# Squared-ReLU MLP on one core: a new start (x in partition halves, first matmuls on half the columns) and blocks in the order A0 A1 B0 A2 B1 A3 B2 B3

## The chip, the core and the metric

The kernel runs on one core of a Trainium2 chip. TensorE (PE in the profile, with PEld for its weight loads) does all matrix products, ScalarE (ACT) and VectorE (DVE) move results out of PSUM, GpSimd (POOL) prepares constants, and SyncE (SP) issues most transfers. The metric is the device time of one execution, in microseconds (us). Lower is better. The kernel before has a median of 292.39 us over three runs (292.11 to 292.75).

## The reference

```python
# B, S, D, F = 1, 2048, 576, 4608; all bf16
h = jnp.einsum("bsd,df->bsf", x, w1) + b1
r = jnp.where(h > 0, h, 0)
out = jnp.einsum("bsf,fd->bsd", r * r, w2) + b2
```

Two matrix products with a squared ReLU between them. Each has 2048 x 576 x 4608 multiply-adds.

## The kernel before, in words

**Blocks and phases.** The 2048 rows of x are cut into four blocks (0 to 3) of 512 rows. For each block, phase A computes the hidden layer transposed: `hT` has 128 partitions, 36 column tiles of F (the loop variable `ft`) and 512 rows of x. Phase B multiplies it with w2 into four row tiles of 128 rows by 576 columns, as two halves of 288 columns, adds b2 and writes them out. Two `hT` buffers exist (`hpool`, L51). The order of the phases is written out by hand at the end of the function (L275 to L291): A0 A1 B0 B1 A2 A3 B2 B3.

**Phase A has two kinds of matmul.** D = 576 is four and a half times 128. For the first four column tiles of F (`a_full`, L180), four matmuls use the whole array with a contraction of 128 (`full`, L194), and the last 64 rows of D are done by two matmuls that run side by side on the lower and upper 64 rows of the array (`pair`, L188 and L190). For the other 32 column tiles (`a_rows`, L164) everything is done by such pairs, with nine contractions of 64 each: L173 on the lower half, L175 on the upper half. Call the first kind full-array and the second kind half-array matmuls. Phase B (L233) is full-array, with 288 columns. In A0 the full-array part comes first and goes contraction by contraction over four PSUM banks (`"k_outer"`, L205); in A1 and A3 the half-array part comes first and `a_full` follows (`"rows_first"`, L197); in A2 `a_full` comes first, bank by bank (`"g_outer"`, L211).

**Transposed x.** Phase A needs x transposed (`xT`, nine windows of 64 or 128 partitions). Blocks 1 to 3 get it by transposing transfers (L120, L121). Block 0 gets it on TensorE: four row tiles `x_sb` are loaded, each is transposed in five 128 x 128 pieces (three into `ta`, L138, two into `tb`, L141 and L142); DVE copies `ta` (L139) and ACT copies `tb` (L143, L144) into `xT`. The first window used, O, is written by DVE's copy; `dup_windows` (L113, L114) then copies windows to the other half of the partitions.

**The start.** TensorE first runs warm-up matmuls on a constant (L61): six of 512 columns and one of 256. SP issues x row tile 0 and x row tile 2, ACT issues row tiles 1 and 3 (L83 to L86, by `load_x`, L70). SP then issues the four parts of `w1n` (L73, the weights of the full-array part of A, one for each contraction `k`), and after them the stream of `w1_h` (L80, w_h in the profile: the weights of the half-array part, first one column tile for each half, then two at a time), the transposing loads of block 1, more of `w1_h`, b2 and w2. POOL makes the identity for the transposes, loads b1 (L94) and then the two halves of `w1n8` (L77, w1n_89 in the profile: the 64 last rows of D for the first four column tiles). All instructions are kept in program order on each engine (`keep`), so TensorE does the 20 transposes of the four row tiles before the first matmul of A0. The transpose of b1 (L151) stands after contraction k = 1 of A0.

**PSUM.** Eight banks: four in `ps_h` (the transposes `ta`, the half-array results, two of the four `a_full` banks) and four in `ps_o` (`tb`, the other two `a_full` banks, phase B). ACT takes an A result out with the ReLU and b1 (L161), DVE squares it into `hT` (L162). DVE adds b2 to a B result (L242), and SP writes it out (L261, the last two halves by L254).

Of the kernel before, what the change touches and what calls it, by code (L numbers as in the profile page):

```python
# [17 lines left out]
def kernel(  # L18
# [9 lines left out]
    nc = tc.nc  # L28
    keep = tc.keep_in_program_order
    P = 128  # L30
    H = 64
    x2 = x.flatten_outer_dims()
# [5 lines left out]
    NK = NC // 2  # L38
    G = 4
# [4 lines left out]
    SB = 512  # L44
# [11 lines left out]

    wps = ps_o.tile([P, 512], FP32, name="wps", tag="po")
    ones = nc.const_aps.tensor(1.0, [P, 512], BF16)
    WARM = [512] * 6 + [256]
    for i, n in enumerate(WARM):  # L60
        keep(nc.tensor.matmul(wps[:, 0:n], lhsT=ones[:, 0:P], rhs=ones[:, 0:n], start=True, stop=True))  # L61

    xs = const.tile([P, RT, D], BF16, name="x_sb")
    w1n = wpool.tile([P, NK, GW], BF16, name="w1n")
    w1n8 = wpool.tile([P, G // 2, P], BF16, name="w1n8")
    w1_h = wpool.tile([P, NC, FH], BF16, name="w1_h")
    w1_v = w1.rearrange("(c p) f -> p c f", p=H)

    def load_x(eng, rt):
        keep(eng.dma_start(out=xs[:, rt, :], in_=x2[rt * P:(rt + 1) * P, :]))  # L70

    def load_w1n(eng, k):
        keep(eng.dma_start(out=w1n[:, k, :], in_=w1[k * P:(k + 1) * P, 0:GW]))  # L73

    def load_w1n8(eng, h):
        src = w1[NK * P:D, 0:GW].rearrange("p (i h f) -> p i h f", h=2, f=P)
        keep(eng.dma_start(out=w1n8[h * H:(h + 1) * H, :, :], in_=src[:, :, h, :]))  # L77
# [2 lines left out]
        keep(eng.dma_start(out=w1_h[h * H:(h + 1) * H, :, j0 * P:j1 * P],  # L80
                      in_=w1_v[:, :, GW + h * FH + j0 * P:GW + h * FH + j1 * P]))

    load_x(nc.sync, 0)  # L83
    load_x(nc.scalar, 1)
    load_x(nc.sync, 2)
    load_x(nc.scalar, 3)  # L86
    for k in range(NK):
        load_w1n(nc.sync, k)

    ident = const.tile([P, P], BF16, name="ident")  # L90
    make_identity(nc, ident[:])
    b1_rows = const.tile([P, P], BF16, name="b1_rows")
    nc.gpsimd.memset(b1_rows[:], 0.0)
    nc.gpsimd.dma_start(out=b1_rows[0:NFT, :], in_=b1.rearrange("(ft p) -> ft p", p=P))  # L94
    load_w1n8(nc.gpsimd, 0)
    load_w1n8(nc.gpsimd, 1)
    warm = const.tile([P, 1], FP32, name="warm")
    keep(nc.scalar.activation(out=warm[:], in_=nc.const_aps.tensor(0.0, [P, 1], FP32), func=ACT.Relu))  # L98

    E3, O, SPC, E = 0, 1, 5, 6  # L100
# [53 lines left out]
    hTs = {}  # L154

    def alloc_hT(sb):
        hTs[sb] = hpool.tile([P, NFT, SB], BF16, name="hT", tag="hT")
# [6 lines left out]
    def a_rows(sb, dup_at=None, dup_sb=None):  # L164
        xT = xT_blk[sb]
        for j in range(NJ):
            if j == dup_at:
                dup_windows(dup_sb)
            bx = ps_h.tile([P, SB], FP32, name="ph", tag="ph")
            by = ps_h.tile([P, SB], FP32, name="ph", tag="ph")  # L170
            jc = slice(j * P, (j + 1) * P)
            for i in range(NC):
                keep(nc.tensor.matmul(bx[:], lhsT=w1_h[0:H, LO_C[i], jc], rhs=xT[0:H, LO_W[i], :],  # L173
                                 start=(i == 0), stop=(i == NC - 1)))
                keep(nc.tensor.matmul(by[:], lhsT=w1_h[H:P, UP_C[i], jc], rhs=xT[H:P, UP_W[i], :],  # L175
                                 start=(i == 0), stop=(i == NC - 1)))
            evac_h(sb, bx, G + j)
            evac_h(sb, by, G + NJ + j)

    def a_full(sb, order):  # L180
        xT = xT_blk[sb]
        banks = []
        for g in range(G):
            pool, tag = (ps_o, "po") if g < 2 else (ps_h, "ph")
            banks.append(pool.tile([P, SB], FP32, name="pn", tag=tag))

        def pair(i, start, stop):
            keep(nc.tensor.matmul(banks[2 * i][:], lhsT=w1n8[0:H, i, :], rhs=xT[0:H, SPC, :],  # L188
                             start=start, stop=stop))
            keep(nc.tensor.matmul(banks[2 * i + 1][:], lhsT=w1n8[H:P, i, :], rhs=xT[H:P, E3, :],  # L190
                             start=start, stop=stop))

        def full(g, k, start, stop):
            keep(nc.tensor.matmul(banks[g][:], lhsT=w1n[:, k, g * P:(g + 1) * P], rhs=xT[:, O + k, :],  # L194
                             start=start, stop=stop))

        if order == "rows_first":  # L197
            for i in (1, 0):
                pair(i, True, False)
            for g in (2, 3, 0, 1):  # L200
                for k in range(NK):
                    full(g, k, False, k == NK - 1)
                evac_h(sb, banks[g], g)
        else:
            if order == "k_outer":  # L205
                for k in range(NK):
                    for g in range(G):
                        full(g, k, k == 0, False)
                    if k == 1:
                        make_b1T()  # L210
            else:  # L211
                for g in (2, 3, 0, 1):
                    for k in range(NK):
                        full(g, k, k == 0, False)
            for i in (1, 0):
                pair(i, False, True)
                evac_h(sb, banks[2 * i], 2 * i)
                evac_h(sb, banks[2 * i + 1], 2 * i + 1)
# [5 lines left out]
    def phase_b(sb, hT, last=False, dups=()):  # L224
        for jj in range(RT):
            if jj < len(dups):
                dup_windows(dups[jj])
            rt = sb * RT + jj
            po = [ps_o.tile([P, 512], FP32, name="po", tag="po") for _ in range(2)]
            o_sb = opool.tile([P, D], BF16, name="o_sb", tag="o_sb")  # L230

            def mmb(i, ft, h):
                keep(nc.tensor.matmul(  # L233
                    po[h][:, 0:DH],
                    lhsT=hT[:, ft, jj * P:(jj + 1) * P],
                    rhs=w2_sb[:, ft, h * DH:(h + 1) * DH],
                    start=(i == 0),
                    stop=(i == NFT - 1),
                ))

            def evac(h):
                keep(nc.vector.tensor_tensor(  # L242
                    out=o_sb[:, h * DH:(h + 1) * DH],
                    in0=po[h][:, 0:DH],
                    in1=b2_bc[:, h * DH:(h + 1) * DH],
                    op=ALU.add,
                ))

            if last and jj == RT - 1:
                for h in range(2):  # L250
                    for i, ft in enumerate(ft_order):
                        mmb(i, ft, h)
                    evac(h)
                    keep(nc.sync.dma_start(out=out2[rt * P:(rt + 1) * P, h * DH:(h + 1) * DH], in_=o_sb[:, h * DH:(h + 1) * DH]))  # L254
                continue
            for i, ft in enumerate(ft_order):
                for h in range(2):
                    mmb(i, ft, h)
            for h in range(2):
                evac(h)  # L260
            keep(nc.sync.dma_start(out=out2[rt * P:(rt + 1) * P, :], in_=o_sb[:]))  # L261
# [18 lines left out]
    a_rows(1)  # L280
    a_full(1, "rows_first")
    phase_b(0, hTs[0], dups=(2, 3))
    phase_b(1, hTs[1])
    alloc_hT(2)
    a_full(2, "g_outer")
    a_rows(2)
    alloc_hT(3)
    a_rows(3)
    a_full(3, "rows_first")
    phase_b(2, hTs[2])  # L290
    phase_b(3, hTs[3], last=True)  # L291

# [29 lines left out]
```

## Time and profile before

| what | value |
| --- | --- |
| median of three runs | 292.39 us (292.11 to 292.75) |
| the profiled execution, own time | 292.11 us |
| its span | 290.3 us, so 1.8 us lie outside the span |
| PE busy | 285.7 us, 2409 recorded matmuls |
| ACT busy, DVE busy | 94.2 us, 81.5 us |
| first matmul of the program (warm-up) | 0.78 us |
| first transpose of x | 3.51 us |
| first full-array matmul of A0 (L194) | 5.71 us |
| first half-array matmul of A0 (L173) | 9.75 us |
| last matmul ends | 287.3 us |

The profile's page has the busy time of each engine, the span in 40 slices, the chain of work that ended last, the costliest groups of instructions by line, and the transfers. Besides the page, the timeline (instructions in order of time; neighbours of one line are merged, "x3" means three), a table of busy time and transferred bytes by stretch of time, and the list of transfers with their time from issue to landing are used below. In the timeline a line holds start, duration, engine, source line, operation, tiles and the number of merged instructions; in brackets the idle time of that engine before it and what ended it. Matmuls overlap in the pipeline: the distance from one start to the next is the pace, the duration of one is longer. A few matmul records are missing in a trace: 61 of the 64 of L194 are there.

### The profile page before, as it was taken

To read this page: it belongs to the slowest core of one execution; us is meant where nothing else is said; L and a number is where in the kernel's file an instruction comes from. 1 tells how busy PE (TensorE), PEld (TensorE's weight loads), DVE (VectorE), ACT (ScalarE), POOL (GpSimd) and SP (SyncE) were. 2 spreads that over 40 slices of the span, in tenths; PEclk is the share of its full clock that TensorE was granted. 3 is DMA by queue.
4 is the path that set the end of the run, shared out by engine and by line. 5 is a ranking of instruction groups with operands and counts; after the bars stand their busy time and mean duration, and the time that the engine had idled before them with its cause. 6 is when DMAs were issued, how large, how long until landed. Compare 5 with 4: busy or idle time off the path is not lost.

```text
span 290.3 us, 5455 instructions
## 1 busy us (share of the span) xinstructions
PE 285.7 (98%) x2409; PEld 178.0 (61%) x2412; DVE 81.5 (28%) x189; ACT 94.2 (32%) x154; POOL 2.7 (1%) x10
## 2 busy tenths in 40 slices
PE   8999999999999999999999999999999999999995
PEld 4444444444677777777744444444447777777774
DVE  3344544444531011110025444444440111100111
ACT  4566666666400000000027666666670000000000
POOL 3000000000000000000000000000000000000000
PEclk9999999999999999999999999999999999999999
DMA  7999999900000000000000000000000000000000
GB/s 203 214 212 177 255 357 265 164 1 2 0 23 0 23 20 20 23 3 20 20 23 0 3 0 2 0 2 0 2 0 2 20 24 20 21 2 23 20 20 24
DMA packets 27096, 16.05 MB, mean 55 GB/s; under 512 B 11028, under 2 KB 27040, under 8 KB 27072
## 3 DMA queue, kind: packets, MB, share of 16 engines
q1 hardware_dynamic: 26688, 15.32, 23.9%
q8 instruction: 19, 0.31, 0.4%
q10 hardware_dynamic: 288, 0.30, 0.3%
q0 software_dynamic: 96, 0.07, 0.1%
q14 instruction: 5, 0.04, 0.0%
HBM read 11.36 MB, written 2.36 MB: 47 GB/s over the span
## 4 chain that ended last, share of the span: by engine, by line
PE 98%; ACT 0%; issue 0%; DVE 0%
PE po L233 49%; PE ph L173 42%; PE pn L194 5%; PE wps L61 1%; PE ph L175 1%; PE pn L188 1%; PE ta L138 0%; ACT xTw L143 0%; DVE o_sb L242 0%; ACT xTw L144 0%; PE tb L141 0%; PE tb L142 0%; PE b1T_ps L151 0%; PE pn L190 0%
## 5 line engine op out<-in xcount | busy, mean ns | idle before, releaser
L233 PE MATMUL po<-w_sb,hT 128*128 128x288 bf16 x1152 | 141.4, 286 | 0.0
L233 PEld LDWEIGHTS <-hT 128*128 128x128 bf16 x1152 | 112.7, 98 | 28.8
L173 PE MATMUL ph<-xTw,w_h 64*128 64x512 bf16 x576 | 124.6, 376 | 0.0
L175 PE MATMUL ph<-xTw,w_h 64*128 64x512 bf16 x576 | 124.6, 376 | 0.0
L173 PEld LDWEIGHTS <-w_h 64*128 64x128 bf16 x576 | 54.1, 94 | 68.3
L161 ACT ACTIVATE r<-ph,b1T 128x512 bf16<-128x512 f32 x128 | 81.1, 685 | 41.6 <-PE ph L175 41.6
L162 DVE TENSOR_TENSOR hT<-r 128x512 bf16<-128x512 bf16 x144 | 61.2, 426 | 77.3 <-ACT r L161 76.7
L175 PEld LDWEIGHTS <-w_h 64*128 64x128 bf16 x576 | 54.1, 94 | 0.0
L242 DVE TENSOR_TENSOR o_sb<-po,b_bc 128x288 bf16<-128x288 f32 x32 | 13.3, 453 | 123.9 <-PE po L233 123.9
L161 ACT ACTIVATE r<-pn,b1T 128x512 bf16<-128x512 f32 x16 | 10.3, 688 | 78.8 <-PE pn L190 77.5
L194 PE MATMUL pn<-xTw,w1n 128*128 128x512 bf16 x61 | 14.0, 379 | 0.8 <-ACT xTw L143 0.4
L194 PEld LDWEIGHTS <-w1n 128*128 128x128 bf16 x64 | 6.0, 98 | 8.0 <-issue 1.4
L61 PE MATMUL wps<-const-bfloat16-1.0 128*128 128x512 bf16 (+1 forms) x7 | 2.9, 594 | 0.8 <-PEq L306 0.8
L113 DVE COPY xTw<-xTw 64x2048 bf16<-64x2048 bf16 x4 | 2.8, 690 | 0.4 <-ACT xTw L144 0.3
L114 DVE COPY xTw<-xTw 64x2048 bf16<-64x2048 bf16 x4 | 2.7, 687 | 0.1
L139 DVE COPY xTw<-ta 128x384 bf16<-128x384 bf16 x4 | 1.3, 358 | 4.2 <-PE ta L138 4.2
L188 PE MATMUL pn<-xTw,w1n_89 64*128 64x512 bf16 x8 | 2.4, 379 | 0.0
L190 PE MATMUL pn<-xTw,w1n_89 64*128 64x512 bf16 x8 | 2.4, 379 | 0.0
L61 PEld LDWEIGHTS <-const-bfloat16-1.0 128*128 128x128 bf16 x7 | 0.9, 135 | 2.1 <-issue 2.1
L98 ACT ACT_TABLE_LOAD x1 | 1.3, 1283 | 1.7 <-PEq L306 1.7
L138 PE MATMUL ta<-ident,x_sb 128*128 128x128 bf16 x12 | 1.6, 265 | 0.0
L143 ACT COPY xTw<-tb 128x128 bf16<-128x128 bf16 x4 | 1.1, 282 | 1.2 <-PE tb L142 1.1
(21 smaller groups left out, 10.2 us busy)
## 6 DMA issues: line engine op xcount, KB each, us to landing
w_sb<-in_w_dram SPq DMA_DIRECT2D x6, 864.0 KB, 11.4
w_h<-in_w_dram SPq DMA_DIRECT2D x14, 288.0 KB, 7.4
out_dram<-o_sb SPq DMA_DIRECT2D x15, 144.0 KB, 1.8
w_h<-in_w_dram SPq DMA_DIRECT2D x4, 144.0 KB, 4.1
w1n<-in_w_dram SPq DMA_DIRECT2D x4, 128.0 KB, 4.0
x_sb<-in_x_dram ACTq DMA_DIRECT2D x2, 144.0 KB, 3.0
x_sb<-in_x_dram SPq DMA_DIRECT2D x2, 144.0 KB, 2.8
b_bc<-in_b_dram SPq DMA_DIRECT2D x1, 144.0 KB, 7.6
```

What stands on the lines that cost most here:

```text
L61: keep(nc.tensor.matmul(wps[:, 0:n], lhsT=ones[:, 0:P], rhs=ones[:, 0:n], start=True, stop=True))
L113: keep(nc.vector.tensor_copy(out=xT[0:H, SPC:SPC + 4, :], in_=xT[H:P, E3:E3 + 4, :]))
L114: keep(nc.vector.tensor_copy(out=xT[H:P, SPC:SPC + 4, :], in_=xT[0:H, O:O + 4, :]))
L161: keep(nc.scalar.activation(out=r[:], in_=bank[:], func=ACT.Relu, bias=b1T[:, ft:ft + 1], scale=1.0))
L162: keep(nc.vector.tensor_tensor(out=hTs[sb][:, ft, :], in0=r[:], in1=r[:], op=ALU.mult))
L173: keep(nc.tensor.matmul(bx[:], lhsT=w1_h[0:H, LO_C[i], jc], rhs=xT[0:H, LO_W[i], :], start=(i == 0), stop=(i == NC - 1)))
L175: keep(nc.tensor.matmul(by[:], lhsT=w1_h[H:P, UP_C[i], jc], rhs=xT[H:P, UP_W[i], :], start=(i == 0), stop=(i == NC - 1)))
L188: keep(nc.tensor.matmul(banks[2 * i][:], lhsT=w1n8[0:H, i, :], rhs=xT[0:H, SPC, :], start=start, stop=stop))
L190: keep(nc.tensor.matmul(banks[2 * i + 1][:], lhsT=w1n8[H:P, i, :], rhs=xT[H:P, E3, :], start=start, stop=stop))
L194: keep(nc.tensor.matmul(banks[g][:], lhsT=w1n[:, k, g * P:(g + 1) * P], rhs=xT[:, O + k, :], start=start, stop=stop))
L233: keep(nc.tensor.matmul(po[h][:, 0:DH], lhsT=hT[:, ft, jj * P:(jj + 1) * P], rhs=w2_sb[:, ft, h * DH:(h + 1) * DH], start=(i == 0), stop=( ...
L242: keep(nc.vector.tensor_tensor(out=o_sb[:, h * DH:(h + 1) * DH], in0=po[h][:, 0:DH], in1=b2_bc[:, h * DH:(h + 1) * DH], op=ALU.add,))
```

## The change

Five edits. (1) The warm-up has four matmuls of 512 columns in place of six. (2) Row tiles 0 and 1 of x are loaded as halves of 64 partitions, the lower half issued by SP and the upper half by ACT; row tiles 2 and 3 are then both issued by SP. (3) `w1n8` is issued by SP after `w1n`, in place of by POOL after b1. (4) In A0 the four matmuls of contraction k = 0 become eight of 256 columns: first the four banks on the columns of row tiles 0 and 1, then the four banks on the columns of row tiles 2 and 3. (5) The phases come in the order A0 A1 B0 A2 B1 A3 B2 B3, and in A3 the full-array part comes first (`"g_outer"`) and the half-array part follows.

```diff
-    WARM = [512] * 6 + [256]
+    WARM = [512] * 4 + [256]
...
+    def load_x_half(eng, rt, h):
+        keep(eng.dma_start(out=xs[h * H:(h + 1) * H, rt, :], in_=x2[rt * P + h * H:rt * P + (h + 1) * H, :]))
+
...
-    load_x(nc.sync, 0)
-    load_x(nc.scalar, 1)
+    for rt in range(2):
+        load_x_half(nc.sync, rt, 0)
+        load_x_half(nc.scalar, rt, 1)
     load_x(nc.sync, 2)
-    load_x(nc.scalar, 3)
+    load_x(nc.sync, 3)
     for k in range(NK):
         load_w1n(nc.sync, k)
+    load_w1n8(nc.sync, 0)
+    load_w1n8(nc.sync, 1)
...
-    load_w1n8(nc.gpsimd, 0)
-    load_w1n8(nc.gpsimd, 1)
...
             if order == "k_outer":
-                for k in range(NK):
+                for half in range(2):
+                    hc = slice(half * (SB // 2), (half + 1) * (SB // 2))
                     for g in range(G):
-                        full(g, k, k == 0, False)
+                        keep(nc.tensor.matmul(banks[g][:, hc], lhsT=w1n[:, 0, g * P:(g + 1) * P],
+                                              rhs=xT[:, O, hc], start=(half == 0), stop=False))
+                for k in range(1, NK):
+                    for g in range(G):
+                        full(g, k, False, False)
                     if k == 1:
                         make_b1T()
...
     phase_b(0, hTs[0], dups=(2, 3))
-    phase_b(1, hTs[1])
     alloc_hT(2)
     a_full(2, "g_outer")
     a_rows(2)
+    phase_b(1, hTs[1])
     alloc_hT(3)
+    a_full(3, "g_outer")
     a_rows(3)
-    a_full(3, "rows_first")
     phase_b(2, hTs[2])
     phase_b(3, hTs[3], last=True)
```

## The prediction

> **What bounds the kernel now.** I read the page's busy times first, then its chain of work that ended last.
>
> ```profile
> span 290.3 us, 5455 instructions
> ...
> PE 285.7 (98%) x2409; PEld 178.0 (61%) x2412; DVE 81.5 (28%) x189; ACT 94.2 (32%) x154; POOL 2.7 (1%) x10
> ...
> PE 98%; ACT 0%; issue 0%; DVE 0%
> ```
>
> TensorE is busy for 98% of the span, and the chain is TensorE for 98%. No matmul of A or B is taken out, so only TensorE's holes and the pace of the few microseconds around them can move. The second view is the timeline of the first 10 us.
>
> ```profile
> 0.78 2.93 PE L61 MATMUL wps<-const-bfloat16-1.0 128*128 128x512 bf16 x7 [0.78 <-PEq L306]
> ...
> 3.46 0.30 PEld L138 LDWEIGHTS <-x_sb 128*128 128x128 bf16 x3 [0.44 <-DMA x_sb<-in_x_dram]
> 3.51 0.52 PE L138 MATMUL ta<-ident,x_sb 128*128 128x128 bf16 x3
> ...
> 4.61 0.96 DVE L139 COPY xTw<-ta 128x384 bf16<-128x384 bf16 x3 [0.17 <-PE ta L138]
> ...
> 4.84 0.33 PE L138 MATMUL ta<-ident,x_sb 128*128 128x128 bf16 x3
> ...
> 5.06 0.22 PE L142 MATMUL tb<-ident,x_sb 128*128 128x128 bf16 x1
> ...
> 5.71 1.89 PE L194 MATMUL pn<-xTw,w1n 128*128 128x512 bf16 x8 [0.43 <-ACT xTw L143]
> ...
> 7.49 1.89 PE L194 MATMUL pn<-xTw,w1n 128*128 128x512 bf16 x8
> ...
> 9.31 0.39 PE L188 MATMUL pn<-xTw,w1n_89 64*128 64x512 bf16 x1
> ```
>
> Three things are to be seen. Warm-up ends as x arrives (3.46). Three transposes take 0.52 us at 3.51 and 0.33 at 4.84: one step is 107 ns until about 4.5 and 56 ns after. Then TensorE is idle for 0.43 us. The bracket names an ACT copy that ended at 5.70, but window O is written by DVE's four L139 copies, which end at 4.61 + 0.96 = 5.57; the weight load starts at 5.68, 0.11 later. I take DVE as the releaser. The third view is the table by stretch; its last column is GB/s.
>
> ```profile
> 2.00:3.00 1.00, 1.00 (x4) 0.42 (x3) 0.00 (x0) 0.99 (x2) 1.00 (x3) 1.00 0.84 268
> 3.00:4.00 1.00, 1.00 (x8) 0.56 (x7) 0.00 (x0) 0.15 (x1) 0.38 (x1) 1.00 1.10 369
> 4.00:5.00 1.00, 1.00 (x16) 1.00 (x14) 0.75 (x3) 0.68 (x4) 0.00 (x0) 1.00 1.06 270
> ```
>
> The transfers are saturated from 2 us on, with a share of one or more. Before 2.0 only 22 kB are moved. So in this stretch a load lands when the bytes ahead of it are through, plus a lag. The granted clock stands at 1.00 all along and does not show the slow steps before 4.5. The fourth view is a change from half-array to full-array matmuls, in A1.
>
> ```profile
> 72.13 0.38 PE L188 MATMUL pn<-xTw,w1n_89 64*128 64x512 bf16 x1
> 72.13 0.38 PE L190 MATMUL pn<-xTw,w1n_89 64*128 64x512 bf16 x1
> 72.67 0.59 PE L194 MATMUL pn<-xTw,w1n 128*128 128x512 bf16 x2 [0.16 <-issue]
> ```
>
> Pairs are 0.215 us apart elsewhere. Here 0.54 us pass, but only 15 of the 16 matmuls of this `a_full` are recorded, so one step of 0.216 is in it: 0.54 - 0.215 - 0.216 = 0.11 us for the change of kind. The other way, the eight L194 from 7.49 end at 9.38, so the last starts at 9.38 - 0.38 = 9.00; the pair follows at 9.31, 0.31 later in place of 0.216: 0.10, with 0.01 more before the next pair.
>
> **Edits 1 and 2, x and the warm-up.** One row tile is 147 kB. Row tiles 0 and 1 (295 kB) were through at about 3.0 (22 + 268 = 290 kB) and landed at 0.74 + 2.7 = 3.44 on SP and 0.74 + 2.9 = 3.64 on ACT, so the lag is 0.4 to 0.6 us. Now the first 147 kB are all row tile 0: 2.0 + 125/268 = 2.47, landing 2.9 to 3.1. The other end is no gain, 3.44, if ACT's half comes no sooner than a whole tile did. I take 3.1, nearest to ACT's slower row. The warm-up's steps are 0.427 us, two fewer end it at 3.51 - 0.85 = 2.66. It was hidden behind x, so this saves nothing by itself and leaves a hole of 0.44. From 3.1, 13 transposes fit before 4.5 at 107 ns and seven follow at 56 ns: the last step ends at 4.89 (before: 5.12). Row tile 3 must be there at 4.61. By bytes it is at 3.0 + 300/369 = 3.81 plus the lag, 4.2 to 4.4, as before (issued 1.2, landed 3.2 later). By its issue, now fourth on SP at about 2.05, and that 3.0 to 3.2, it is 5.05 to 5.25. I take the bytes, since later issues landed no later than bytes allow; the other end costs up to 0.6.
>
> The Trainium skill, "DMA: Bandwidth & Descriptors", section "Rules for kernel authors", speaks against the split: two transfers to disjoint partition halves serialize, and one 128-partition transfer is to be used. By it the halves as such gain nothing, and row tile 0 would profit only from going ahead of row tile 1; if that too gave nothing, the sum would be 0.1 to 0.2 us smaller.
>
> **Edit 4, the half columns.** The first four matmuls need only row tiles 0 and 1 and w1n 0. w1n 0 landed at 1.65 + 3.3 = 4.95; its issue goes to 0.74 + 4 x 0.45 = 2.55 but the bytes ahead are the same, so 4.95 stays, and the half starts at 5.0. Four steps of 0.108 (half of 0.216) end at 5.43. The second half waits for DVE's copy of row tile 3: its `ta` is done at 4.72 + 0.22 = 4.94, DVE is free at about 5.02, the copy takes 0.36, the lag is 0.11: 5.49. Then four more steps, so k = 1 starts at 5.92. Before it was 5.71 + 4 x 0.216 = 6.57. **Gain 0.65.** What is late next: w1n 1, which landed at 6.03, when POOL's w1n8 was between; that is gone, so I cost it at nothing (0.1 otherwise). w1n 2 and 3 (6.6 and 7.3) are wanted at 6.8 and 7.7. By the instruction order of the changed program the third w1n issue waits for a half of row tile 0 to land (3.1), and SP is not there before 3.45.
>
> **Edit 3, SP's queue.** SP issues two more x loads and two w1n8 ahead of w_h, at 0.45 us each (four w1n took 1.85): w_h starts at about 5.25 in place of 3.61. TensorE wants the first two w_h at its first half-array weight load, 9.54 - 0.65 = 8.9. They landed 4.1 us after issue, at 7.7 and 8.5, but behind queued w1n. Without a queue a load of the same size took 2.7: 7.95 and, one issue step of 0.7 later, 8.65. At 4.1 they land at 9.35 and 10.05 and cost up to 1.15. By the bytes, all that goes ahead of w_h is through at 6.0 both ways (22 + 268 + 369 + 270 + 267 = 1196 kB; x, w1n, w1n8 and b1 are 1.19 MB), so I take the short end with 0.1 to 0.3 us of delay. The sixth w_h (7.21 + 5.5 = 12.7) is the tightest: wanted at about 13.5 before, so the spare time is 0.75. With the delay the gain that can be kept is about 0.55. I use **0.55**.
>
> **Edit 5, the order.** Changes of kind before: A0 and A2 to half-array, A1 and A3 to full-array, four. After: A0, A2, A3 to half-array, and into A1's `a_full`, B1 and B2 to full-array, six. One more of each: 0.11 + 0.11 = **0.22 lost**. Into B itself the trace has no such change; it could be nothing or, at most, twice the row. All else is hidden: the `hT` buffers that A2 and A3 write come free with the last matmul of B0 and B1, and their first result comes some 4 us later (A2: L194 at 146.46, last pair at 150.24); from B to `a_full` TensorE goes on without a hole (L233 ends its steps at 146.46).
>
> **Sum:** -0.55 + 0.22 = -0.33, with 0.01 for the four added matmuls. The profiled execution, 292.11, becomes 291.78; it lies 0.28 below the median, so the median becomes 292.05.
>
> **The rivals.** *Better, 291.7:* changes into B cost half, and w_h comes without delay: -0.65 + 0.11 = -0.54, to -0.75 if x is at 2.9 too. For it: bytes speak for early landings. Against: 0.1 us of spare time for w_h.
>
> *Transfers go by issue, not by bytes, 292.4 to 293.1:* row tile 3 at 5.05 takes 0.4 of the gain (+0.0), w_h at 4.1 makes it -0.65 + 1.15 + 0.22 = +0.72. For it: SP alone now carries the issues. Against: the share at one or more.
>
> *The slow steps last longer, 293.1, the slower side:* the place is the hole from 2.66 to 3.1. Steps halved at 4.5, 3.7 us after the first matmul, with TensorE at work without a hole. If the hole starts that count anew, steps halve at 3.1 + 3.7 = 6.8, and 2.3 us run at half pace: +1.15. Then w_h is wanted late enough: -0.65 + 1.15 + 0.22 = +0.72. It decides as soon as the hole counts as rest at all. Against it: the hole is 12% of that time, and after 4.5 a longer one (0.43) left the pace alone.
>
> "TensorE: Matmul & The Clock Gate", Part 1 of the skill, has the clock released after a busy window of some 3.4 us that runs freely and is not started by the kernel. By it a hole does not restart the count, but a window that misses costs another 3.4 us at half pace, 1.7 us as an estimate, and single runs would differ. No row here shows the window.
>
> **How the numbers follow.** 0.2% is 0.58 us, about what a measurement of this kernel can tell from no change. The likeliest case (0.40; -0.33, own range 291.75 to 292.35) is faster by more in 0.06. Better (0.22): faster 0.17, within 0.05. By issue (0.14): within 0.10, slower 0.04. Slow steps (0.24): slower 0.20, within 0.04. So faster 0.23, same 0.53, slower 0.24. The range goes from 291.5 (better at -0.65, less the 0.3 by which runs fall below their median) to 293.2 (slow steps with 0.1 on top); about 0.06 are left out below and 0.08 above.
>
> **What would show it.** In the changed profile: first transpose at 3.1; 56 ns steps from 4.5 (at 6.8: the slow-step rival); four L213 matmuls at 5.0 and four at 5.5; L198 at 5.9; the first half-array matmul at 9.1 to 9.2 (9.75 before), and no hole ahead of the third column tile; 0.1 us at each change into B1 and B2. It is wrong if that half-array matmul is not before 9.5, or if B1 and B2 start after holes much over 0.1.

## The result and the profile after

The changed kernel takes 294.82 us in the median (294.67 to 295.17, six runs), the kernel before 292.49 beside it (292.06 to 292.75): a ratio of 1.0084 [1.0071, 1.0097]. It is slower by 2.3 us. The forecast was 292.05, no measurable change, and the result lies above its range (291.5 to 293.2).

The profiled execution took 294.68, 1.8 of it outside the span. The page of the changed kernel has these lines:

```profile
span 292.9 us, 5462 instructions
...
PE 287.1 (98%) x2411; PEld 178.2 (61%) x2414; DVE 81.6 (28%) x189; ACT 94.0 (32%) x154; POOL 1.5 (1%) x8
...
PE 93%; SPq 3%; DMA 2%; issue 0%; DVE 0%
PE po L242 48%; PE ph L177 21%; PE ph L179 20%; PE pn L198 3%; DMA w_h<-in_w_dram 2%; SPq L83 1%; SPq L76 1%; SPq L70 0%; SPq L80 0%; PE pn L192 0%; SPq L73 0%; DVE o_sb L251 0%; PE pn L194 0%
```

The busy shares tell nothing: 98% as before. The chain does. Before, it was TensorE from the start (98%). Now it begins with SP's queue (SPq 3%) and one transfer of w_h (2%), together 5% of 293 us, some 15 us. So something arrives at about 15.7 us that holds TensorE, and the cause is what SP issued ahead of it. The beginning of this chain for the changed kernel (start, duration, link; "..." marks lines left out):

```profile
0.74 0.58 SPq L70
...
1.39 0.81 SPq L70
...
3.37 0.43 SPq L76
...
10.01 5.66 DMA w_h<-in_w_dram
...
15.71 0.39 PE ph L179
```

Here each SP line is one issue: 0.58 and 0.81 for the two halves of x on SP, 0.43 for the first w1n. The lines between have 0.60 and 0.43 for the whole row tiles, 0.65 and 0.61 for w1n8, and w_h after these.

Lines have moved: the transposes L138 are now L142, full-array L194 is L198, the half columns are L213, half-array L173 and L175 are L177 and L179, the issues of w1n, w1n8 and w_h are L76, L80 and L83. The timeline of the changed kernel, SP's issues and TensorE's first work of each kind:

```profile
0.74 1.46 SPq L70 DMA_DIRECT2D x_sb<-in_x_dram  x2
...
3.37 1.85 SPq L76 DMA_DIRECT2D w1n<-in_w_dram  x4
3.38 0.48 PE L142 MATMUL ta<-ident,x_sb 128*128 128x128 bf16 x3 [0.52 <-DMA x_sb<-in_x_dram]
...
5.27 1.30 SPq L80 DMA_DIRECT2D w1n_87<-in_w_dram  x2
...
5.91 0.31 PE L146 MATMUL tb<-ident,x_sb 128*128 128x128 bf16 x1
...
6.15 1.14 PEld L213 LDWEIGHTS <-w1n 128*128 128x128 bf16 x8 [0.20 <-DMA w1n<-in_w_dram]
...
6.62 5.40 SPq L83 DMA_DIRECT2D w_h<-in_w_dram  x8
...
7.42 1.03 PE L198 MATMUL pn<-xTw,w1n 128*128 128x512 bf16 x4
...
10.60 0.38 PE L177 MATMUL ph<-xTw,w_h 64*128 64x512 bf16 x1
```

The same of the kernel before, SP alone, to 12 us:

```profile
0.74 0.85 SPq L70 DMA_DIRECT2D x_sb<-in_x_dram  x2
1.65 1.85 SPq L73 DMA_DIRECT2D w1n<-in_w_dram  x4
3.61 9.36 SPq L80 DMA_DIRECT2D w_h<-in_w_dram  x11
```

Read SP's lines from top to bottom: it hardly rests. Two loads of 64 partitions cost 1.46 us where two loads of 128 partitions had cost 0.85 before; two w1n8 (64 partitions too) cost 1.30. w1n is issued from 3.37 (before: 1.65), w_h from 6.62 (before: 3.61). On TensorE the first half columns start at 6.16, and the bracket names w1n, with 0.20. But they could not have started much earlier: all transposes stand ahead of them in TensorE's order, row tile 3 of x landed only at 5.46, and its last transpose (L146, at 5.91) made way at about 6.02. So both loads, x and w1n, were late. The first half-array matmul starts at 10.60 (before: 9.75). The same engine around 15 us:

```profile
14.58 0.38 PE L177 MATMUL ph<-xTw,w_h 64*128 64x512 bf16 x1
...
15.71 0.39 PE L179 MATMUL ph<-xTw,w_h 64*128 64x512 bf16 x1 [0.76 <-DMA w_h<-in_w_dram]
```

From 14.58 to 15.71 are 1.13 us where 0.22 is the pace: the sixth w_h, issued at 10.01, landed 5.66 later. Before, the corresponding load had landed at 12.7. The table by stretch of the changed kernel, whose last two columns are DMA share and GB/s:

```profile
2.00:3.00 1.00, 0.86 (x3) 0.15 (x1) 0.00 (x0) 1.00 (x1) 0.11 (x1) 1.00 0.66 191
3.00:4.00 1.00, 0.62 (x5) 0.45 (x5) 0.11 (x1) 0.45 (x2) 0.00 (x0) 1.00 0.90 222
4.00:5.00 1.00, 0.85 (x9) 0.76 (x9) 0.52 (x2) 0.49 (x3) 0.00 (x0) 1.00 0.89 254
...
7.00:8.00 1.00, 1.00 (x8) 0.66 (x7) 0.97 (x2) 0.00 (x0) 0.00 (x0) 1.00 0.28 67
```

In 2 to 5 us 667 kB are moved (191 + 222 + 254); before it was 907 (268 + 369 + 270). The share is below one in each row, and in 7 to 8 us it falls to 0.28 (67 GB/s): the transfers wait for issues, they are not saturated.

**Where the 2.3 us lie** (last matmul ends at 289.62, before 287.33: 2.29):

| place | us |
| --- | --- |
| first half-array matmul, 9.75 to 10.60 | +0.85 |
| hole at 10.60, the lower array half runs one step ahead of the upper, which waits for the second w_h (10.85) | +0.08 |
| hole at 14.58, the sixth w_h | +0.92 |
| the lag of one half pays one more step at the end of A1's pairs | +0.20 |
| two more changes of matmul kind | +0.19 |
| sum | +2.24 |

The row on the changes of kind is read in the timeline at the first change into B1:

```profile
148.13 0.38 PE L179 MATMUL ph<-xTw,w_h 64*128 64x512 bf16 x1
148.43 0.42 PE L242 MATMUL po<-w_sb,hT 128*128 128x288 bf16 x2
```

From 148.13 to 148.43 are 0.30 us in place of a step of 0.215, some 0.09 for the change of kind.

**Behind the last matmul** the changed kernel loses a little more. From there to the end of the span are 3.01 us before (290.34 - 287.33) and 3.29 now (292.92 - 289.62). In both, the last store to `out` lands 2.1 us after the last matmul. SP ends the program with a row of waits for transfers, one after the other, and the trace shows the wait for the last store as the last of them before, as the second of six now. What stands behind it comes on top. From the list of SP's waits, the line on the last store (in all, times, longest), first of the kernel before, then of the changed kernel, then of the kernel that has the partition halves alone (below):

```profile
SPq L317 <- DMA out_dram<-o_sb: 0.4, 1, 0.4
```

```profile
SPq L326 <- DMA out_dram<-o_sb: 0.8, 1, 0.8
```

```profile
SPq L321 <- DMA out_dram<-o_sb: 1.3, 1, 1.3
```

In the last of these SP waits for the store first of all, and 3.85 us pass behind the last matmul. Which wait it is differs between kernels with other loads at the start, and it repeats where a kernel was profiled twice (3.01 and 3.02; 3.84 and 3.84). So up to 0.84 us of a difference between two kernels can have nothing to do with TensorE.

### The profile page after: what moved, and what is told of

It is laid out like the page before. It is cut to its first block, busy times and chain, and to the rows that moved or that the text cites. A ratio compares the mean times of both kernels' runs of the same rounds, so it can differ in the third digit from the quotient of the medians.

```text
span 292.9 us, 5462 instructions
## 1 busy us (share of the span) xinstructions
PE 287.1 (98%) x2411; PEld 178.2 (61%) x2414; DVE 81.6 (28%) x189; ACT 94.0 (32%) x154; POOL 1.5 (1%) x8
## 4 chain that ended last, share of the span: by engine, by line
PE 93%; SPq 3%; DMA 2%; issue 0%; DVE 0%
PE po L242 48%; PE ph L177 21%; PE ph L179 20%; PE pn L198 3%; DMA w_h<-in_w_dram 2%; SPq L83 1%; SPq L76 1%; SPq L70 0%; SPq L80 0%; PE pn L192 0%; SPq L73 0%; DVE o_sb L251 0%; PE pn L194 0%
## 5 line engine op out<-in xcount | busy, mean ns | idle before, releaser
L179 PE MATMUL ph<-xTw,w_h 64*128 64x512 bf16 x576 | 125.0, 376 | 0.8 <-DMA w_h<-in_w_dram 0.8
L177 PE MATMUL ph<-xTw,w_h 64*128 64x512 bf16 x576 | 125.1, 376 | 0.0
L179 PEld LDWEIGHTS <-w_h 64*128 64x128 bf16 x576 | 54.0, 94 | 35.4 <-DMA w_h<-in_w_dram 2.2
L177 PEld LDWEIGHTS <-w_h 64*128 64x128 bf16 x576 | 54.0, 94 | 34.2
L198 PE MATMUL pn<-xTw,w1n 128*128 128x512 bf16 x57 | 13.3, 379 | 0.3 <-issue 0.2
L198 PEld LDWEIGHTS <-w1n 128*128 128x128 bf16 x60 | 5.8, 98 | 6.6 <-issue 0.4
L61 PE MATMUL wps<-const-bfloat16-1.0 128*128 128x512 bf16 (+1 forms) x5 | 2.1, 579 | 0.8 <-PEq L315 0.8
L142 PE MATMUL ta<-ident,x_sb 128*128 128x128 bf16 x12 | 2.0, 302 | 0.7 <-DMA x_sb<-in_x_dram 0.5
L194 PE MATMUL pn<-xTw,w1n_87 64*128 64x512 bf16 x8 | 2.4, 380 | 0.0
L142 PEld LDWEIGHTS <-x_sb 128*128 128x128 bf16 x12 | 1.0, 123 | 2.0 <-DMA x_sb<-in_x_dram 1.9
```

What stands on the lines that cost most here:

```text
L142: keep(nc.tensor.transpose(ta[:, i, :], xs[:, j, i * P:(i + 1) * P], ident[:]))
```

## The experiments

The theory after seeing the result: SP issues its loads one after the other, each for 0.4 to 0.8 us, and what is issued late lands late; the halves of x and w1n8 push w1n and w_h back, and the result is this push. The rivals: the transfers of 64 partitions are themselves bad (the bytes come slower); TensorE's slow steps last longer because of the short warm-up; the new order of the phases costs more than the two changes of kind. Unless said otherwise, a kernel computes the full output, and ratios are against the kernel before in the same session (medians 292.57 to 292.65; the ratio is not the quotient of two medians). The table sets off what lies behind the last matmul. Its last column is an estimate: the difference of the medians, less that of one profiled execution of each kernel.

| kernel | median against before, us | behind the last matmul | the rest, estimate |
| --- | --- | --- | --- |
| the changed kernel | +2.33 | +0.28 | +2.05 |
| order alone | +0.21 | 0 | +0.2 |
| start alone | +2.43 | +0.29 | +2.1 |
| half columns alone | -0.47 | 0 | -0.5 |
| half columns, w1n on two queues | +0.10 | 0 | +0.1 |
| short warm-up alone | +0.57 | 0 | +0.6 |
| long warm-up in the changed kernel | +2.42 | +0.29 | +2.1 |
| partition halves alone | +2.20 | +0.84 | +1.4 |
| column halves | +1.74 | +0.83 | +0.9 |
| w1n8 on POOL | +3.36 | +0.82 | +2.5 |
| w1n8 on POOL, long warm-up | +1.93 | +0.83 | +1.1 |
| whole row tiles in the changed kernel | +1.32 | +0.25 | +1.1 |
| w1n8 on SP alone | +0.91 | +0.66 | +0.25 |
| two loads of 64 partitions | +1.27 | +0.81 | +0.5 |
| two loads of 128 partitions | +1.06 | +0.81 | +0.25 |

**Order alone.** The kernel before with only edit 5.

```diff
-    phase_b(1, hTs[1])
     alloc_hT(2)
     a_full(2, "g_outer")
     a_rows(2)
+    phase_b(1, hTs[1])
     alloc_hT(3)
+    a_full(3, "g_outer")
     a_rows(3)
-    a_full(3, "rows_first")
```

> The kernel before with the new order of phases alone (edit 5). Theory (the start is what costs): two changes of kind more at 0.10 each, so +0.2 us, 292.7, and the start as before (first half-array matmul at 9.75). Rival (the order is the main cost, by holes or a lower pace later on): +1 us or more.

Measured: 292.86, 1.0004 [0.9994, 1.0014]. Last matmul 287.49 with a start 0.06 earlier than before, so +0.2. The order is not the cause.

**Start alone.** The changed kernel with the order of before (edits 1 to 4 remain).

> The changed kernel with the order of phases of before (edits 1 to 4 alone). Theory: +2.1 us, 294.6: first half-array matmul at 10.6 (+0.85), holes for w_h near 10.6 and 14.6 (+1.2 with the lag of one step that they leave). Rival (the order is the main cost): +1 us or less.

Measured: 295.08, 1.0077 [1.0055, 1.0099]; as slow as the changed kernel. Nearly all of the loss comes with edits 1 to 4. In the profiled execution the slow steps lasted to about 9.4, the first half-array matmul came at 12.10, 1.5 later than in the changed kernel, and yet TensorE ended at 289.67: there was no hole for w_h left. The late w_h and the late start of the half-array part hide each other.

**Half columns alone.** The kernel before with only edit 4.

```diff
-                for k in range(NK):
+                for half in range(2):
+                    hc = slice(half * (SB // 2), (half + 1) * (SB // 2))
                     for g in range(G):
-                        full(g, k, k == 0, False)
+                        keep(nc.tensor.matmul(banks[g][:, hc], lhsT=w1n[:, 0, g * P:(g + 1) * P],
+                                              rhs=xT[:, O, hc], start=(half == 0), stop=False))
+                for k in range(1, NK):
+                    for g in range(G):
+                        full(g, k, False, False)
...
```

> The kernel before with edit 4 alone, the eight matmuls of 256 columns. Theory: it covers most of the 0.43 us hole: first half at 5.13, second half when DVE's last copy is done (5.7), k = 1 at about 6.14 in place of 6.57: -0.4 us, 292.1. Rival (the hole is only moved, since w1n 1 landed at 6.03 and the second half still waits for DVE): -0.1 to 0.

Measured: 292.18, 0.9983 [0.9971, 0.9995]: faster by 0.5 us than the kernel before, and the best version found. Its timeline on TensorE (L209 is the half columns here, L194 the rest):

```profile
4.90 1.05 PE L209 MATMUL pn<-xTw,w1n 128*128 128x256 bf16 x8
...
6.14 1.04 PE L194 MATMUL pn<-xTw,w1n 128*128 128x512 bf16 x4 [0.19 <-DMA w1n<-in_w_dram]
```

The half columns start at 4.90 in place of 5.71; the bracket shows what is late next, w1n 1, by 0.19. (In this execution the steps were fast from 3.5 on, which is part of its own gain.)

**Half columns with w1n on two queues.** To take that wait away, w1n 1 and 3 are issued by ACT.

```diff
-        load_w1n(nc.sync, k)
+        load_w1n(nc.sync if k % 2 == 0 else nc.scalar, k)
```

> The kernel before with the half columns, and parts 1 and 3 of w1n issued by ACT in place of SP. Theory (in the kernel with half columns alone, k = 1 waited for w1n 1 until 6.1): w1n 1 is issued 0.45 earlier and lands before 5.9, and w_h goes out 0.9 earlier: 0.1 to 0.3 below the kernel with half columns alone, 291.9. Rival (bytes, not issues, set when w1n 1 lands; ACT's table load comes later and delays its copies): no change against half columns alone, 292.2, or worse.

Measured: 292.67, 1.0000 [0.9987, 1.0013]. The gain is gone: w1n 0 landed only at 6.27 and w1n 1 at 6.67. A likely reading is that w1n 1 now went beside w1n 0, and that the first, which alone is wanted at once, came later by it; with one execution profiled, and w1n 0 at 4.86 to 5.60 in kernels that left its loads alone, this is not shown. The theory, 0.1 to 0.3 us below half columns alone, fell.

**Short warm-up alone.** The kernel before with only edit 1.

```diff
-    WARM = [512] * 6 + [256]
+    WARM = [512] * 4 + [256]
```

> The kernel before with edit 1 alone: warm-up ends at 2.66, x lands at 3.46, so TensorE rests 0.8 us. Theory that the rest delays the halving of the steps: steps stay at 107 and 427 ns until about 3.5 us after x, near 7.0 in place of 4.5, +1.0 to +1.2 us, 293.6. Rival (the rest does not matter, steps halve at 4.5): no change within 0.2 us.

Measured: 293.22 (292.3 to 294.5), 1.0017 [0.9997, 1.0037]: unclear, some 0.6 us and a wide spread. In the profiled execution the steps were still slow at the last transpose, 5.5, and fast from 6.2 on (before: from 4.5).

**Long warm-up in the changed kernel.** Edit 1 undone, all else changed.

> The changed kernel with the long warm-up of before. Theory (the sixth w_h sets the end, so a clock that comes later is hidden behind it): first half-array matmul up to 0.4 earlier, but the same wait until 15.7: 294.8 within 0.2. Rival (the late halving of the steps is a part of the loss): -0.4 us or more.

Measured: 295.05, 1.0079 [1.0061, 1.0096], no better than the changed kernel. The steps halved at 4.7, nearly as early as before. w1n 0 landed at 6.76 in this execution (6.11 in the changed kernel), so the first half-array matmul came no earlier, at 10.88; and then TensorE met the same late load. The timeline of this kernel:

```profile
15.84 0.39 PE L179 MATMUL ph<-xTw,w_h 64*128 64x512 bf16 x1 [0.70 <-DMA w_h<-in_w_dram]
```

So in the changed kernel the warm-up costs nothing that could be seen, since whatever TensorE gained ahead of 15.8 it would give back there.

**Partition halves alone.** The kernel before with x loaded as in edit 2, except that ACT still issues row tile 3.

```diff
+    def load_x_half(eng, rt, h):
+        keep(eng.dma_start(out=xs[h * H:(h + 1) * H, rt, :], in_=x2[rt * P + h * H:rt * P + (h + 1) * H, :]))
...
-    load_x(nc.sync, 0)
-    load_x(nc.scalar, 1)
+    for rt in range(2):
+        load_x_half(nc.sync, rt, 0)
+        load_x_half(nc.scalar, rt, 1)
```

> The kernel before with row tiles 0 and 1 of x as partition halves on SP and ACT; row tile 2 stays on SP, 3 on ACT, w1n8 on POOL, the long warm-up. Theory (an issue of 64 partitions costs about 0.6 to 0.8 us, one of 128 some 0.43, and the first bytes come 0.5 later): w1n is issued from 2.7 in place of 1.65, w_h from 4.7 in place of 3.61; the sixth w_h lands near 13.9, just late: +0.3 to +0.6 us. Rival (only the number of loads on SP counts, 0.45 each): w1n from 2.1, no hole: 0 to -0.2.

Measured: 294.83, 1.0080 [1.0052, 1.0108]: as slow as the whole change. But 0.84 of the 2.2 us lie behind the last matmul (0.28 in the changed kernel), so on TensorE the halves alone cost some 1.4 us, the whole change some 2.05. The first two issues took 1.47 us. The issue of w1n and TensorE's first full-array matmuls in the timeline of this kernel:

```profile
2.90 1.85 SPq L76 DMA_DIRECT2D w1n<-in_w_dram  x4
...
6.97 1.25 PE L198 MATMUL pn<-xTw,w1n 128*128 128x512 bf16 x5 [0.85 <-DMA w1n<-in_w_dram]
```

w1n is issued 1.25 later than before (2.90 against 1.65) and w1n 0 lands at 6.92 in place of 4.95, 1.97 later. So 1.25 of the delay is the queue; the other 0.7 is a longer way from issue to landing (4.0 in place of 3.3), which the queue does not explain. Chance may: in five executions of kernels that leave these loads as before (the kernel before twice, order, half columns and short warm-up alone) it was 3.2 to 3.9. No hole for w_h follows here; the first half-array matmul comes at 11.03, 1.27 later than before, and TensorE ends 1.27 later. The Trainium skill, "DMA: Bandwidth & Descriptors", section "Rules for kernel authors", says not to split a load into two transfers to disjoint partition halves but to use one of 128 partitions. The advice holds here: two such splits made the kernel slower, by some 1.4 us before the last matmul ends. That the two transfers serialize, the trace does not show: the halves of row tile 0, issued together by SP and ACT, landed at 3.27 and 3.06.

**Column halves.** The same, but each half has all 128 partitions and 288 columns: the same number of loads and bytes, other shape.

```diff
-        keep(eng.dma_start(out=xs[h * H:(h + 1) * H, rt, :], in_=x2[rt * P + h * H:rt * P + (h + 1) * H, :]))
+        keep(eng.dma_start(out=xs[:, rt, h * DH:(h + 1) * DH], in_=x2[rt * P:(rt + 1) * P, h * DH:(h + 1) * DH]))
```

> As the kernel with partition halves, but each half has all 128 partitions and 288 of the 576 columns: the same bytes and the same number of loads on each queue. Theory (64 partitions are what makes an issue dear): issues of 0.40 to 0.45, first bytes at 1.6 as before, w1n from 2.1: 0 within 0.2 us. Rival (two small loads at once on two queues are dear whatever their shape): as with partition halves, +0.3 to +0.6.

Measured: 294.37 (293.37 to 296.3), 1.0071 [1.0046, 1.0096]. Two views of it, SP's first issues in the timeline, and then x's whole row tiles in the list of transfers (count, size, us from issue to landing):

```profile
0.74 0.86 SPq L70 DMA_DIRECT2D x_sb<-in_x_dram  x2
```

```profile
x_sb<-in_x_dram SPq DMA_DIRECT2D x1, 144.0 KB, 4.6
...
x_sb<-in_x_dram ACTq DMA_DIRECT2D x1, 144.0 KB, 4.8
```

On the issue the theory was right: 0.43 each in place of 0.73, and w1n goes out from 2.12. On the time it was wrong: 0.83 of the 1.74 us lie behind the last matmul, but some 0.9 are left. In the profiled execution, the slowest of the ten, row tiles 2 and 3 took 4.6 and 4.8 us to land, TensorE stood still from 5 to 6 us, and steps that had been fast were slow again from 7.4 to 10.8. The same kernel again:

> The kernel with column halves, a second look. If its late loads are systematic: row tiles 2 and 3 land after 6 again, w1n 0 near 6.6. If they were chance: row tiles 2 and 3 before 4.6, w1n 0 at 5.0 to 5.5.

Measured: 293.45 in one run. Row tiles 2 and 3 now landed at 4.95 and 5.19 in place of 6.2 and 6.4, w1n 0 at 5.49, the first half-array matmul came at 10.26 in place of 13.12. TensorE ended at 287.84, as in the second execution of the kernel before (287.91, below): the 0.75 us between the times of these two lie behind the last matmul (3.84 against 3.02). So the very late tiles were chance; that six loads of x on two queues tend to make the last two late, whatever their shape, is not excluded.

**w1n8 on POOL.** The changed kernel with edit 3 undone.

```diff
-    load_w1n8(nc.sync, 0)
-    load_w1n8(nc.sync, 1)
...
+    load_w1n8(nc.gpsimd, 0)
+    load_w1n8(nc.gpsimd, 1)
```

> The changed kernel with w1n8 issued by POOL again. Theory (SP's queue sets when the sixth w_h lands, and that sets the end): w_h from 5.27 in place of 6.62, the sixth lands near 14.3 in place of 15.67, TensorE wants it at 14.5: about -1.2 us, 293.6. Rival (the late start of A0 or the order sets the end): within 0.3 of the changed kernel, 294.8.

Measured: 295.99, 1.0101 [1.0070, 1.0132], the slowest of all, and 0.54 more of it than in the changed kernel lie behind the last matmul. w_h is issued from 5.30 and its hole is gone, as the theory has it. But x and w1n landed later (row tiles 2 and 3 at 5.49 and 5.82, w1n 0 at 6.87), and the steps stayed slow until 11.4; TensorE in the timeline of this kernel:

```profile
6.92 1.89 PE L213 MATMUL pn<-xTw,w1n 128*128 128x256 bf16 x8
...
13.18 0.38 PE L177 MATMUL ph<-xTw,w_h 64*128 64x512 bf16 x1
```

The same eight half columns took 1.42 in the changed kernel, from 6.16. The expectation was missed, and two causes remained, the pace and the late w1n 0.

**w1n8 on POOL, long warm-up.** The same with edit 1 undone as well.

> The kernel with w1n8 on POOL again, now with the long warm-up as well. Theory (there w_h was in time, and what made it slow was that the steps halved only at 11.3): steps halve by about 5, first half-array matmul near 11.0 in place of 13.2, no hole for w_h: 294.0, some 2 us below that kernel. Rival (x and w1n that land late are the whole loss, the clock is no part): within 0.5 of it, 295.5 to 296.

Measured: 294.50, 1.0072 [1.0046, 1.0098]. The median is 1.5 below the former, though the two intervals overlap. In the profiled executions steps halve at 5.35 in place of 11.4, the first half-array matmul comes at 10.92 in place of 13.18, and no hole follows. So in that execution the pace was 2 us, with no late w_h to hide it; whether the short warm-up or chance made it so, the medians do not settle. What is left is the late w1n 0 (6.81). The kernel with the long warm-up and w1n8 on SP (above) differs from this one only in w1n8: there TensorE ends at 289.75, here at 288.75. That is what the theory asked for, some 1 us for two issues fewer ahead of w_h, though the medians differ by 0.55 only, since 0.54 more lie behind the last matmul here.

**Whole row tiles in the changed kernel.** Edit 2 replaced by four whole loads, three of them on SP.

```diff
-    for rt in range(2):
-        load_x_half(nc.sync, rt, 0)
-        load_x_half(nc.scalar, rt, 1)
+    load_x(nc.sync, 0)
+    load_x(nc.scalar, 1)
```

> The changed kernel with row tiles 0 and 1 loaded whole again, 0 by SP and 1 by ACT; row tiles 2 and 3 and w1n8 stay on SP, the rest is as changed. Theory (the halves make up some 1.3 us of SP's delay, the rest comes from row tile 3 and w1n8): w_h from about 5.35, the sixth lands near 14.4, which now sets the end: 14.4 - 13.6, plus 0.2 for the order and up to 0.2 for the lag of one step, 293.5. Rival (halves are harmless): 294.8, as changed.

Measured: 293.89, 1.0049 [1.0036, 1.0063]. w_h is issued from 5.45, 1.17 earlier than in the changed kernel; the sixth lands at 14.24, and the holes at 10.60 and 14.58 are gone. The first half-array matmul comes at 10.59, and the end at 288.38. That is 1.24 us before the changed kernel's end: the two holes and the lag (0.08 + 0.92 + 0.20 = 1.20). The two intervals, [1.0036, 1.0063] and [1.0071, 1.0097], do not overlap. So the halves account for these holes, about 1 us of 2.3. What is left before the last matmul, 1.04 in this execution, is the first half-array matmul, 0.84 later than before, and the order. Ahead of it stand row tile 3, now the third load on SP (landed at 5.57), w1n 0 (5.95), and slow steps until 7.0; how much each has of the 0.84 was not separated, as no kernel with whole row tiles has the long warm-up.

**w1n8 on SP alone.** The kernel before with only edit 3.

> The kernel before with edit 3 alone, w1n8 on SP after w1n. Theory (each of the two issues takes 0.65 on SP): w_h from 4.9 in place of 3.61; the sixth lands near 13.9 in place of 12.7 and is wanted at 13.5: +0.2 to +0.5 us, 293.0. Rival (w1n lands earlier without POOL's packets between, and the bytes set w_h): 0 to -0.2.

Measured: 293.48, 1.0032 [1.0015, 1.0048]. The two issues take 0.72 and 0.59, w_h starts at 5.22 in place of 3.61, and there is a hole of 0.17 at 33.80 plus the lag of 0.21. In the profiled execution the first half-array matmul also came 0.74 later (w1n 0 landed at 5.46, the steps halved at 6.6). Of the median's 0.91, 0.66 lie behind the last matmul; the 0.25 left are less than the 0.5 us by which the interval reaches to either side, so a loss on TensorE shows in the trace and is not shown by the times. The sixth w_h landed at 14.26, 1.53 later than before, for an issue 1.39 later (8.60 against 7.21).

**Issue time by itself.** The kernel before with two extra loads on SP ahead of w1n, into a tile that nobody reads, with 4 bytes for each of 64 partitions. They carry next to no bytes, so their bytes cannot matter. A second kernel has 128 partitions.

```diff
+    scr = const.tile([P, 8], BF16, name="scr")
+    for i in range(2):
+        keep(nc.sync.dma_start(out=scr[0:H, 2 * i:2 * i + 2], in_=x2[0:H, 0:2]))
```

> The kernel before with two extra loads on SP ahead of w1n, 64 partitions of 4 bytes each, into a tile that nobody reads. Theory (SP's issue time is the loss, and 64 partitions cost 0.6 or more): w1n issued from 2.9 in place of 1.65, w_h from 4.9; w1n 0 lands near 6.0, A0 starts 0.6 to 1.0 later, the sixth w_h is just late: +0.8 to +1.4 us. Rival (the halves' own bytes and packets make the loss): within 0.3 of before.

> The same with 128 partitions of 4 bytes each. Theory (an issue of 128 partitions costs 0.43): w1n from 2.55, w_h from 4.5; w1n 0 lands near 5.5, before the second half of x is copied: 0 to +0.5 us, less than with 64. Rival (the number of loads, or their packets, is what counts): as with 64.

Measured: 293.89, 1.0039 [1.0025, 1.0054] with 64 partitions, and 293.68, 1.0043 [1.0030, 1.0056] with 128. The timeline of the former, first SP and then TensorE (here L176 and L178 are the half-array matmuls):

```profile
1.69 1.20 SPq L89 DMA_DIRECT2D scr<-in_x_dram  x2
...
5.00 8.25 SPq L80 DMA_DIRECT2D w_h<-in_w_dram  x10
```

```profile
33.55 0.38 PE L176 MATMUL ph<-xTw,w_h 64*128 64x512 bf16 x1
...
34.24 0.39 PE L178 MATMUL ph<-xTw,w_h 64*128 64x512 bf16 x1 [0.32 <-DMA w_h<-in_w_dram]
```

Two loads of 256 bytes each make the kernel slower by 1.3 us. They take SP 1.20 us; w_h starts 1.39 later, and TensorE meets it with holes of 0.21 at 13.90 and 0.48 as late as 33.55. So issue time alone moves the stream of weights and opens holes. But 0.81 of the 1.3 us lie behind the last matmul, and so do 0.81 of the 1.06 with 128 partitions; some 0.5 and 0.25 are left, which the times hardly tell from nothing (the intervals reach about 0.4 to either side). The size of the issues' cost is not shown by these two. With 128 partitions the two issues take 0.90, and w1n starts at 2.60. That the wider loads cost less in time, as expected, is not shown: the two intervals overlap nearly wholly.

**The kernel before, once more,** to see how far one kernel varies in its start.

> The kernel before, a second look. If landing times repeat: x at 3.4 to 4.4, w1n 0 at 4.9, sixth w_h at 12.7, all within 0.3, and only the moment at which the steps halve differs (4.5 then). If they are chance: w1n 0 or a w_h off by 0.5 or more.

Measured: 292.70 in one run. TensorE's last row tile of x in its timeline:

```profile
5.11 0.52 PE L138 MATMUL ta<-ident,x_sb 128*128 128x128 bf16 x3
```

The three transposes took 0.33 in the execution that the prediction used, 0.52 here: the steps halved at about 6.4, not 4.5, and the first half-array matmul came at 10.34, not 9.75. w1n 0 landed at 5.30, not 4.94. The same kernel differs by 0.6 us here by chance, so a single profiled execution is good for mechanisms, and only the medians for sizes. Where a landing time is compared between two kernels, 0.7 us of it can be such chance: in the five executions that left its loads as before, w1n 0 landed at 4.86 to 5.60.

## Why the prediction was wrong, by its own steps

**What bounds the kernel** was read rightly, TensorE, and nearly all of the loss is in its holes and first microseconds. But "saturated from 2 us on", "with a share of one or more", was more than its rows had (0.84 in 2 to 3 us), and the change itself undid it: SP issues longer for the same bytes, and the share fell to 0.66 to 0.90. How late these loads land then depends on their issue. The stream of w_h begins late by it and does not make that up: from the fourth to the ninth its loads land 1.4 to 1.5 us apart (1.4 before), though issued 0.7 apart.

**Edits 1 and 2.** The first transpose was put at 3.1; it came at 3.38. Row tile 0 landed at 3.24 by its slower half, 3.42 before. Row tile 3 was taken at 4.2 to 4.4 "by bytes", with 5.05 to 5.25 by its issue; it was issued at 2.90 in place of 2.05 and landed at 5.46. Here the wrong end was taken.

**Edit 4.** The half columns themselves did what was said, as the run with them alone shows (0.9983 [0.9971, 0.9995], -0.5 of the -0.65). In the changed kernel they stood at 6.16 in place of 5.0, because the transposes of row tile 3 kept TensorE until about 6.02 in place of 4.89, and w1n 0 landed at 6.11 in place of 4.95. The issue of w1n 0 was put at 2.55 and came at 3.37; "the bytes ahead are the same, so 4.95 stays" is the sentence that failed.

**Edit 3 is the step that failed most,** and in two ways. First, its cost: "at 0.45 us each" was taken from w1n, a load of 128 partitions. Issues of 64 partitions took 0.58 and 0.81 (x), 0.65 and 0.61 (w1n8). w_h was put at 5.25 and came at 6.62; of the 3.0 us against before, 1.7 are x and 1.3 w1n8. The right row stood in the trace of before: w_h's own loads have 64 partitions, and their first three issues took 2.08 us, 0.69 each. The prediction used 0.7 for them two sentences later, and did not carry it to x and w1n8, which have as many partitions. With 0.69 for the four issues of 64 partitions and 0.45 for six others w_h would have been put at 0.74 + 2.76 + 2.7 = 6.2. Second, its overlap: even the 1.64 us by which it did put the issue of w_h later were turned into "0.1 to 0.3 us of delay", since the bytes were to set the landing. They did not. The sixth w_h was issued 2.80 later than before and landed 2.94 later (15.67); and in the two kernels whose w_h was issued near the 5.25 of the prediction (5.22 with w1n8 on SP alone, 5.45 with whole row tiles) it landed at 14.26 and 14.24, 1.5 later than before. So of the sum's terms the 0.1 to 0.3 was wrong with either issue time. The sixth w_h, put at 0.75 of spare time, became a hole of 0.92 even though TensorE came 0.85 later.

**Behind the last matmul** the sum has no term, and no reason for that; there the changed kernel lost 0.28.

**Edit 5** was right: two more changes of kind, 0.22 predicted, 0.19 measured in the changed kernel, 0.2 in the run with the order alone. A change into B costs about as much as one into `a_full`, as was assumed.

**The rivals.** "Transfers go by issue" had the direction, but 292.4 to 293.1 was too low, since it used 0.45 for each issue and left the sixth w_h out. "The slow steps last longer" had the moment nearly right: steps halved at 7.0, and the rival said 6.8. Yet it was not what set the time: with the long warm-up they halve at 4.7, and the kernel is no faster, as the sixth w_h holds it at 15.8. Nor is its mechanism shown, a count that the hole starts anew: the kernel before, without any hole in the warm-up, had its steps halve at 4.5 once and at 6.4 once.

**What stays open.** The loads that follow the halves sometimes land later than their issue explains (w1n 0 takes 4.0 us after partition halves alone and 4.5 and 3.4 in two executions after column halves, 2.7 in the changed kernel, 3.2 to 3.9 with the loads of before). Whether that is chance, the shape, or w1n8's packets on POOL between them was not settled. Nor was it settled how much of the 0.85 at the first half-array matmul is the slow steps.

## What to carry to other kernels

Count the issues on the queue that feeds a kernel's start, not only the bytes: each load ahead of the first needed one costs its own issue time, here 0.4 to 0.8 us, and moves all loads behind it. A stream of weights with 0.75 us to spare could not take four more such issues, and its hole shows far from the change (at 14.6 and 33.6 us here). Where two delays lie on top of one another, undoing one alone can show nothing (the warm-up here): undo both. And before a small difference is put down to the start, compare what lies behind the last matmul: here it differed by up to 0.84 us, as much as some of the effects looked for.

## What the runs showed of the hardware

- An issue on SP took 0.37 to 0.49 us (once 0.60) with 128 partitions behind another of 128, and 0.57 to 0.82 with 64 partitions (x, w1n8, two loads of 4 bytes for each partition); a load of 128 partitions next behind one of 64 took 0.59 to 0.60. With 4 bytes for each partition it was nearly the same (0.42 to 0.43 and 0.57 to 0.59) as with whole rows: it goes by the form of the load and of the one before it, and hardly by its bytes.
- The moment when TensorE's steps halve is not a property of the kernel. It was 4.5 and 6.4 in two executions of the kernel before, 3.5 with half columns alone, and between 5.5 and 11.4 in the five kernels with the short warm-up; with the long one it was 3.5 to 6.6 where it could be read. So it tends to be later with the short warm-up, though the two ranges meet. The granted clock was 1.00 all along in the changed kernel and the kernel with w1n8 on POOL, slow steps or not. "TensorE: Matmul & The Clock Gate", Part 1 of the Trainium skill, has the clock released after a busy window of some 3.4 us that runs freely. That two executions of one kernel differ by 1.9 us agrees with a window that the kernel does not start; 3.5, which is 2.7 us after the first matmul, is sooner than a whole window of that length. No run here shows the window itself.
- With column halves the granted clock did move: after TensorE had stood still from 5 to 6 us, it was granted 0.69 in 7 to 8 us and 0.50 in 8 to 10.
- Half-array matmuls whose one half waits for weights run on in the other half, one step ahead. The lag of one step stays for the whole stretch and is paid at its end (0.21 us).
- The end of a program can cost 3.0 to 3.85 us behind the last matmul, with the last store landing 2.1 us behind it in all kernels: SP's last waits come one after the other, and those that stand behind the wait for that store add their time.
